# 64-key score blocks, half-height turns and row-wise q and k loads in a fused attention kernel

## The chip, the cores and the metric

The kernel runs on one core of a Trainium2 chip. The time is the device time of one launch in microseconds. The kernel before takes 263.98 us, the median of three runs (263.66 to 265.17).

## The reference

Two attentions in a row, over 8 batches of 576 tokens. The first has 8 heads of 64 and lets a token see only tokens at most 32 away. Its result, 512 wide, is the input of a mixture of four causal attentions ("experts", head width 64) of which each token uses the best two, weighted by a gate.

```python
scores = scale * np.matmul(q, k.transpose(0, 1, 3, 2))
mask = np.abs(pos[:, None] - pos[None, :]) <= window      # window = 32
attn = softmax(np.where(mask, scores, -1e9))
x = (attn @ v)                                            # B, S, 512
logits = x @ w_gate;  topk = best 2 of 4;  w = softmax over the two
for e in range(4):
    q, k, v = x @ wq[e], x @ wk[e], x @ wv[e]
    ye = causal_softmax(scale * q @ k.T) @ v @ wo[e]
    out += (w of e, 0 where e is not chosen) * ye
```

## The kernel before

The program is straight-line code. `ORDER` is a written list of 917 steps; each step has a name, digits for its place in the work (batch first), sometimes a letter after a colon for the engine or the layout, and after an @ the PSUM banks that it uses. A step adds its instructions to the ends of the queues of its engines, so the list is the order on each engine. Semaphores between the engines are put in for the data. A load (`load`, line 184) also waits on its queue until the last TensorE product ahead of it in the list has run, so that a load cannot start earlier than its place.

The steps of the first attention for batch b, head group g (four heads) and half of the queries (288 each):

- `lq`, `lk` load q and k of four heads into a tile of 128 partitions (32 for each head) by 18 tokens by 64. `lv` and `vc` load and copy v.
- `tq`, `tk` (function `turn`, line 288) turn them with VectorE in blocks of 32x32 (line 298), so that the 64 head dimensions lie on partitions as two halves `dh` of 32, for each of four heads: 4 x 32 partitions, tokens along the row. The letters e and f stand for another layout that the list before does not use; t is the layout of the others, issued on ScalarE's queue.
- `sc` (line 323) makes the scores, transposed: keys on partitions, queries along the row, only the blocks that the window touches (`BLK`). Each product has 32 rows of the array (one head, one half `dh`), and the four heads use the four row groups side by side. Two products (`dh` 0 and 1) add up in PSUM. A call has four blocks, one of 128 keys and three of 64, so 32 products. Each fp32 product stands in the trace as two MATMUL records and two LDWEIGHTS records: 64 for each call, in 32 calls. A call uses four of the eight PSUM banks.
- `ex` takes the exponential on ScalarE (line 336, two for each call), `mk` multiplies by the window's mask on VectorE or GpSimd (line 340), `av` multiplies by v, `un` divides by the sums.
- `xt` (line 376) turns the result with TensorE through an identity matrix, in pieces of 128x128, 18 for each batch. `xf` copies it out of PSUM and `xb` casts it to bf16.

The steps of the mixture: `ga`, `gt`, `ge`, `gm`, `gu` are the gate, with small VectorE operations of 20 elements; `pp`/`pe` and `pv`/`ve` the projections and their copies, `ps`/`xe`/`se` scores, exponential and causal mask, `po`/`oe` the product with v, `pt`/`ot` another turn with TensorE (five for each call, the last 64x64), `py`/`ye`/`st` the output product, copy and store.

Lines 179 and 182 are the helpers that issue every product and every TensorE turn, lines 171 and 173 the copies and casts on ScalarE and on VectorE or GpSimd, line 185 every load.

Of the kernel before, what the change touches and what calls it, by code (L numbers as in the profile page):

```python
# [33 lines left out]
    lq200 lk200 xf02:a@0 xb02:v mk1001:g ex1110@4 xt00@6 xf00:a@6 sc110@04 ga0@6 gt0@6 xb00:a ex1101@4 lv10  # L34
    pp001@2 lv12 ex1100@0 mk1100:g lv11 lq210 pp000@0 pe000:v@0 pe001:a@2 pp010@2 pe010:v@2 mk1101:g mk1111:g
    ps003@0 ps000@4 xe003@0 se003 ps002@6 pv00@0 xe000@4 xe002@6 pp011@4 tq200 vc11:g ve00:a@0 pe011:a@4 ps001@6
    xe001@6 tk200 sc200@02 ex2001@2 ps013@4 lv14 xe013@4 mk1110:v lk210 vc10:v lk300 ps010@6 xe010@6 ex2000@0 ge0
    mk2000:g sc201@24 se000 ex2011@4 ex2010@2 se001 ps012@6 tq210 av12@0 mk2011:g un12@0 av10@4 mk2010:g lq300
    pv01@3 xe012@6 ve01:a@3 gm0 lk310 av13@6 av11@0 un10@4 un13@6 un11@0 se012 av14@4 un14@4 tk210 xt11@6 lw3
    xf11:a@6 lv23 xb11:g xt12@0 xf12:v@0 xb12:g xt10@4 lv22 mk2001:g xf10:v@4 xb10:v lv20 ps011@2 xe011@2 sc211@06  # L40
    ex2111@6 ex2110@0 mk2110:v se002 sc210@24 pp110@6 ex2100@2 mk2100:g ex2101@4 lv21 lq310 cw3:g pe110:a@6 gu0
    mk2101:g pp101@2 pe101:a@2 po00@6 pp100@2 tk300 lv24 oe00@6 pp111@4 se011 pt00@6 pe100:v@2 ps102@2 ps103@0
    pe111:a@4 xe102@2 xe103@0 tq300 ga1@7 gt1@7 lq400 ot00:a@6 mk2111:v sc301@24 ex3010@2 ex3011@4 ge1 tk310
    sc300@06 ex3001@6 ps100@2 xe100@2 lk400 tq310 vc21:g se010 av23@4 vc20:g av22@6 un23@4 ex3000@0 pv11@2 un22@6
    ve11:a@2 av20@0 un20@0 av24@7 lk410 un24@7 se013 ps111@4 xe111@4 mk3011:g ps101@2 lv31 xe101@2 av21@0 un21@0
# [12 lines left out]
    xb31:g pp300@4 pt10@0 pp310@6 se211 st02 pt11@1 ot11:a@1 tk600 mk5000:g vc50:g pp301@2 pe301:a@2 xt42@1
    pe310:v@6 pe300:v@4 av42@6 un42@6 av43@2 un43@2 xf42:v@1 st00 ot10:a@0 gm3 py12@0 se203 ye12:a@0 se213
# [28 lines left out]
    ye50:v@0 st50 ps711@6 xe711@6 se711 st51 pv70@2 gu7 pt61@4 ot61:v@4 se703 ve70:a@2 pt60@7 pv71@6 py52@5  # L88
    ye52:a@5 ps710@0 st52 xe710@0 se702 se713 ot60:v@7 py60@2 ye60:a@2 st60 ve71:v@6 po70@6 se710 po71@0 py61@2
    oe70@6 ye61:a@2 pt70@7 st61 py62@6 ye62:a@6 oe71@0 pt71@0 ot71:a@0 ot70:v@7 py70@0 ye70:a@0 py71@6 py72@5 st62  # L90
    ye71:a@6 st70 st71 ye72:v@5 st72
"""


@with_exitstack
def kernel(
# [63 lines left out]
    def two(b0):  # L160
        return PS[:, b0:b0 + 2, :]
# [468 lines left out]
```

## Time and profile before

| | |
|---|---|
| median of three runs | 263.98 us |
| the profiled execution, in all | 264.25 us |
| its span, first to last instruction | 262.5 us |
| TensorE products busy | 228.9 us |
| VectorE busy | 193.2 us |
| ScalarE busy | 147.0 us |
| GpSimd busy | 127.2 us |
| DMA queue of the loads and stores, share of 16 engines | 64.4% |

The profile names the engines PE (TensorE products), PEld (its weight loads), DVE (VectorE), ACT (ScalarE), POOL (GpSimd) and SP (the engine that issues most transfers). A group line gives code line, engine, operation, written and read tiles, shapes, count, then busy time and the mean time of one in ns, then idle time ahead of it and what ended it. For TensorE the shape is rows of the array times columns of the array, then partitions by streamed columns. Busy times of a group count overlapping instructions once, so the mean times count of many products is more than their busy time. A table of stretches gives, for each stretch of the span, its length, the busy time and count of each engine, the granted TensorE clock (1.00 is full), the mean busy share of the DMA engines and GB/s.

### The profile page before, as it was taken

To read this page: it belongs to the slowest core of one execution; us is meant where nothing else is said; L and a number is where in the kernel's file an instruction comes from. 1 tells how busy PE (TensorE), PEld (TensorE's weight loads), DVE (VectorE), ACT (ScalarE), POOL (GpSimd) and SP (SyncE) were. 2 spreads that over 40 slices of the span, in tenths; PEclk is the share of its full clock that TensorE was granted. 3 is DMA by queue.
4 is the path that set the end of the run, shared out by engine and by line. 5 is a ranking of instruction groups with operands and counts; after the bars stand their busy time and mean duration, and the time that the engine had idled before them with its cause. 6 is when DMAs were issued, how large, how long until landed. Compare 5 with 4: busy or idle time off the path is not lost.

```text
span 262.5 us, 11479 instructions
## 1 busy us (share of the span) xinstructions
PE 228.9 (87%) x5013; PEld 183.2 (70%) x5024; DVE 193.2 (74%) x400; ACT 147.0 (56%) x221; POOL 127.2 (48%) x165
## 2 busy tenths in 40 slices
PE   0286999985989999699989999998899989999981
PEld 0165898664768888567878877886688758877650
DVE  2455896759899889998997956986876596667640
ACT  0223416761646557326745677776657657785852
POOL 5019706765686097337967906109734236322400
PEclk9995699999999999999999999999999999999997
DMA  8969989999974598886186798990021520124366
GB/s 166 209 171 180 228 160 211 204 198 226 199 177 138 161 209 176 170 196 162 34 205 201 157 162 159 216 290 15 2 63 42 186 80 2 32 92 157 126 216 208
DMA packets 89362, 40.60 MB, mean 155 GB/s; under 512 B 47072, under 2 KB 84960, under 8 KB 89312
## 3 DMA queue, kind: packets, MB, share of 16 engines
q1 hardware_dynamic: 86752, 38.69, 64.4%
q10 hardware_dynamic: 2560, 1.18, 2.4%
q8 instruction: 39, 0.64, 1.1%
q14 instruction: 11, 0.09, 0.1%
HBM read 30.42 MB, written 9.44 MB: 152 GB/s over the span
## 4 chain that ended last, share of the span: by engine, by line
PE 64%; DVE 16%; DMA 9%; issue 3%; ACT 3%; SPq 2%; POOL 1%; ACTq 0%; DVEq 0%
PE PS L179 57%; PE PS L182 7%; DVE A L340 5%; DMA qn<-in_q_dram 4%; DMA kn<-in_k_dram 4%; SPq L185 2%; ACT A L336 2%; DVE Tkn L298 1%; DVE RG L545 1%; DVE OE L546 1%; DMA out_dram<-Y 1%; DVE XN L368 1%; POOL V L173 1%; DVE Tqn L298 1%; DVE VE L173 1%
## 5 line engine op out<-in xcount | busy, mean ns | idle before, releaser
L179 PE MATMUL PS<-Tqn,Tkn 32*64 32x96 f32 (+5 forms) x2048 | 63.6, 307 | 16.9 <-DVE Tqn L298 11.6
L340 POOL TENSOR_TENSOR A<-A,MASKP 128x576 f32<-128x576 f32 x41 | 59.2, 1458 | 33.1 <-ACT A L336 32.5
L179 PEld LDWEIGHTS PS<-Tqn,Tkn 32*64 32x64 f32 (+1 forms) x2048 | 51.9, 158 | 29.4 <-DVE Tqn L298 12.0
L336 ACT ACTIVATE A<-PS 128x576 f32<-128x576 f32 x64 | 38.9, 650 | 41.0 <-PE PS L179 41.0
L506 ACT ACTIVATE ATE<-PS 128x1024 bf16<-128x1024 f32 x48 | 47.4, 1023 | 8.4 <-PE PS L179 6.8
L511 POOL TENSOR_SCALAR_AFFINE_SELECT ATE<-ATE 128x256 bf16<-128x256 bf16 (+1 forms) x80 | 31.4, 413 | 39.6 <-ACT ATE L506 24.2
L179 PE MATMUL PS<-V,A 128*64 128x65 f32 (+1 forms) x1280 | 39.6, 222 | 3.8 <-DVE XN L368 2.4
L179 PEld LDWEIGHTS PS<-V,A 128*64 128x64 f32 (+1 forms) x1280 | 36.1, 132 | 7.5 <-DVE XN L368 2.9
L173 POOL COPY V<-V 64x2048 f32<-64x2048 f32 (+1 forms) x12 | 21.8, 1820 | 27.3 <-DMA V<-in_v_dram 21.9
L298 DVE STREAM_TRANSPOSE Tkn<-kn 128x576 f32<-128x576 f32 (+2 forms) x36 | 23.2, 686 | 8.4 <-DMA kn<-in_k_dram 7.3
L298 DVE STREAM_TRANSPOSE Tqn<-qn 128x576 f32<-128x576 f32 (+2 forms) x36 | 23.2, 686 | 7.6 <-DMA qn<-in_q_dram 6.6
L340 DVE TENSOR_TENSOR A<-A,MASKP 128x576 f32<-128x576 f32 x23 | 25.3, 1109 | 3.0 <-ACT A L336 3.0
L368 DVE TENSOR_TENSOR XN<-PS,RC 128x512 f32<-128x512 f32 x32 | 22.1, 691 | 1.1
L179 PE MATMUL PS<-WV,XTB 128*128 128x256 bf16 (+1 forms) x192 | 18.8, 255 | 1.1 <-DVE OTT L173 0.8
L179 PE MATMUL PS<-WO,OTT 128*128 128x512 bf16 (+1 forms) x85 | 18.2, 341 | 1.4 <-ACT OTT L171 0.7
L179 PE MATMUL PS<-XTB,WK 128*128 128x288 bf16 x128 | 18.3, 286 | 1.0 <-DVE QKE L173 1.0
L182 PE MATMUL PS<-ident,XN 128*128 128x128 f32 x144 | 18.1, 275 | 1.1 <-DVE XN L373 0.9
L171 ACT COPY Y<-PS 128x1024 f32<-128x1024 f32 (+1 forms) x17 | 13.7, 826 | 9.3 <-PE PS L179 8.3
L179 PE MATMUL PS<-XTB,WQ 128*128 128x288 bf16 x128 | 18.1, 287 | 0.0
L179 PE MATMUL PS<-QKE 64*128 64x64 bf16 (+4 forms) x192 | 16.8, 277 | 1.4 <-DVE QKE L173 1.2
L182 PEld LDWEIGHTS PS<-ident,XN 128*128 128x128 f32 x144 | 15.8, 141 | 3.1 <-DVE XN L373 1.7
L179 PEld LDWEIGHTS <-ATE 128*128 128x128 bf16 x480 | 16.4, 97 | 2.2 <-POOL ATE L511 0.8
(71 smaller groups left out, 279.8 us busy)
## 6 DMA issues: line engine op xcount, KB each, us to landing
V<-in_v_dram SPq DMA_DIRECT2D x32, 256.0 KB, 4.7
out_dram<-Y SPq DMA_DIRECT2D x16, 512.0 KB, 3.8
qn<-in_q_dram SPq DMA_DIRECT2D x56, 144.0 KB, 4.3
kn<-in_k_dram SPq DMA_DIRECT2D x56, 144.0 KB, 4.3
V<-in_v_dram SPq DMA_DIRECT2D x8, 128.0 KB, 4.2
out_dram<-Y SPq DMA_DIRECT2D x16, 64.0 KB, 2.6
kn<-in_k_dram ACTq DMA_DIRECT2D x8, 80.0 KB, 3.5
qn<-in_q_dram SPq DMA_DIRECT2D x8, 80.0 KB, 2.8
```

What stands on the lines that cost most here:

```text
L171: nc.scalar.copy(o, i)
L173: eng(c).tensor_copy(o, i)
L179: last_pe[0] = nc.tensor.matmul(*a, **kw)
L182: last_pe[0] = nc.tensor.transpose(*a)
L185: r = q_.dma_start(o, i)
L298: nc.vector.transpose(T[:, 64 * m0:64 * m1].rearrange("q (m p o) -> q m o p", p=32, o=2), n_[:, 2 * m0:2 * m1, 32 * dh:32 * dh + 32].rearr ...
L336: nc.scalar.activation(AT[(2 * b + g) % NAT_][half][p], two(b0)[:, :, 0:HS], EXP, scale=scale_att)
L340: eng(c).tensor_tensor(out=ap, in0=ap, in1=MASK[:, None, HS * half:HS * half + HS].to_broadcast([128, 2, HS]), op=MULT)
L368: nc.vector.tensor_tensor(out=XN[T // 2][:, T % 2, :].rearrange("p (g h d) -> p g h d", g=2, h=4), in0=u[:, :, :, 0:64], in1=rc[:, :, :, N ...
L506: nc.scalar.activation(chunk(A, ch), two(b0), EXP, scale=scale_moe)
L511: nc.gpsimd.affine_select(ap, ap, pattern=[[0, n], [1, w]], compare_op=IS_GE, fill=0.0, base=0, channel_multiplier=-1)
L545: nc.vector.tensor_tensor(out=rg, in0=GG[b % 2][:, 2 * j:2 * j + 2, :], in1=rg, op=MULT)
```

## The change

Five things change together.

1. `sc`: all blocks have 64 keys, five for each call and so 40 products (80 MATMUL records). Products for the lower half of the partitions (`par` 0) and for the upper half (`par` 1) alternate in an order written out in `SEQ`. Each half of the array columns streams 288 queries for each `dh`.
2. q is loaded in rows of 16 tokens for each partition, with the last 64 tokens in a second transfer of two tokens each (letter x). Its turn is one VectorE instruction of 1,024 elements for each partition and one of 128. The turned q lies in an order (a, p, c), with token 16p + 2a + c, and `sc` reads its queries through that order (`tokens`): pairs of tokens side by side, the next pair 72 elements on.
3. k is loaded in rows of 18 tokens, one transfer of 4,608 bytes for each partition (letter e, or f on ScalarE's queue for batch 0). Its turn is two instructions of 576 elements that write with a step of 18 elements.
4. `xt` turns pieces of 64 partitions by 128, two for each piece of before, into two PSUM banks; `xf` copies from there. The last turn of `pt` is a full 128x128 one.
5. The list is another order of the same 917 steps, with other banks. Letters move some copies: on VectorE `pe` goes from 14 to 9, `xb` from 7 to 1, `xf` from 12 to 10, `ye` from 7 to 4, `ve` from 5 to 4, `ot` from 8 to 11, `mk` from 23 to 25. On ScalarE `pe` goes from 18 to 23, `ye` from 17 to 20, `xf` from 12 to 14, `ot` from 8 to 5. On GpSimd `xb` goes from 10 to 15 and `mk` from 41 to 39.

```diff
@@ -25,70 +25,71 @@
 ORDER = """
-    s_mask s_pads lq100 lk011:t tk011:t lk001:t tk001:t lq011 lq001 tq011 lq002 lk012:t lk002:t lq012 s_ones
-    sc010@02 lv02 lk100 lv01 lv03 s_warm tq001 sc000@46 ex0101@2 ex0001@6 mk0001:g ex0000@4 lv00 s_ident mk0101:g
-    tk002:t tk012:t tq002 sc001@24 ex0011@4 mk0011:g mk0000:g tq012 sc011@46 ex0111@6 tq100 tk100 mk0111:g lq110
-    ex0100@0 ex0110@4 vc00:v ex0010@2 mk0010:v lk110 sc101@06 mk0110:v ex1011@6 tq110 ex1010@0 mk1010:v lv04 lw1
-    sc100@24 vc01:g av02@0 tk110 lv13 ex1001@4 un02@0 mk0100:g av01@4 un01@4 av00@6 un00@6 lw0 ex1000@2 mk1000:v
-    cw0:g av03@2 av04@0 mk1011:g un04@0 sc111@46 un03@2 ex1111@6 cw1:v xt02@0 lw2 cw2:g xt01@2 xf01:v@2 xb01:v
...
+    s_pads s_ones lq012:x lk011:f tq012:x tk011:f lq011:x tq011:x lk012:f tk012:f lk002:f tk002:f lq001:x s_ident
+    tq001:x lq002:x lk001:f lv01 sc010@02 s_warm ex0101@2 lq100:x sc011@46 tq002:x ex0111@6 s_mask mk0111:g
+    lk100:e tk001:f sc000@26 ex0001@6 mk0001:v mk0101:g lv00 ex0100@0 ex0110@4 mk0110:v ex0000@2 mk0100:g lk110:e
+    mk0000:g sc001@06 tk100:e lv03 ex0010@0 mk0010:g lk200:e lv02 tq100:x sc100@02 ex0011@6 mk0011:g ex1001@2
+    vc00:a tk110:e lv04 lq110:x lw1 vc01:g sc101@46 ex1010@4 mk1001:v ex1000@0 lq200:x tk200:e tq110:x ex1011@6
+    av03@2 un03@2 av00@0 un00@0 av01@6 un01@6 av04@4 un04@4 lw0 cw1:g av02@2 un02@2 sc111@06 xt00@4 ex1110@0
+    tq200:x lw2 mk1011:g ex1111@6 xt02@2 lv11 xf02:a@2 xb02:a xt01@0 xf01:v@0 xb01:g sc110@26 cw0:v xf00:a@4
+    xb00:a lv12 ex1101@6 mk1101:v cw2:g ga0@4 gt0@4 ex1100@2 mk1111:v mk1100:g lv13 ge0 pp000@0 lv14 pp001@2
+    pe000:v@0 lv10 vc11:g sc200@46 ex2000@4 pe001:v@2 pp010@0 pe010:v@0 mk1010:v ps002@4 lq210:x gm0 ex2001@6
+    mk2001:g ps001@2 xe001@2 lk210:e vc10:g pp011@6 pe011:a@6 pv00@0 xe002@4 lv22 sc201@26 ve00:a@0 ex2010@2
...
@@ -125,7 +126,9 @@
     PS = psum.tile([128, 8, 512], F32, name="PS")
     NAT = {nm: many(NNAT, [128, 18, 64], F32, nm) for nm in ("qn", "kn")}
 
-    QKT = {nm: [many(2, [128, S], F32, f"T{nm}{g}") for g in range(2)] for nm in ("qn", "kn")}
+    QKT = {nm: many(2, [128, 2, S], F32, "T" + nm) for nm in ("qn", "kn")}
+
+    LAY = {}
     VSB = many(2, [128, 8, H, 65], F32, "V")
 
     AT = [[many(2, [128, 2, HS], F32, f"A{i}{h}") for h in range(2)] for i in range(NAT_)]
@@ -263,21 +266,23 @@
         copy(c, WO, WST[3].rearrange("p (j x) -> p j x", x=512))
 
 
-    PARTS = [(0, 9), (0, 5), (5, 9)]
 
     def load_qk(nm, src, b, g, part, c):
         t = NAT[nm][(2 * b + g) % NNAT]
-        queue = nc.scalar if c in ("f", "t") else nc.sync
+        queue = nc.scalar if c in ("f", "y") else nc.sync
+        s_ = src[b, 4 * g:4 * g + 4]
         if c in ("e", "f"):
             o0, o1 = ((0, 18), (0, 9), (9, 18))[part]
             load(t[:, o0:o1, :].rearrange("p o d -> p (o d)"),
-                 src[b, 4 * g:4 * g + 4].rearrange("h (p o) d -> (h p) o d", o=18)[:, o0:o1, :].rearrange("p o d -> p (o d)"),
+                 s_.rearrange("h (p o) d -> (h p) o d", o=18)[:, o0:o1, :].rearrange("p o d -> p (o d)"), queue)
+        else:
+            o0, o1 = ((0, 16), (0, 8), (8, 16))[part]
+            load(t[:, o0:o1, :].rearrange("p o d -> p (o d)"),
+                 s_[:, 0:512, :].rearrange("h (p o) d -> h p o d", o=16)[:, :, o0:o1, :].rearrange("h p o d -> h p (o d)"),
                  queue)
-        else:
-            m0, m1 = PARTS[part]
-            for h in range(4):
-                load(t[32 * h:32 * h + 32, 2 * m0:2 * m1, :].rearrange("p (m o) d -> p m (o d)", o=2),
-                     src[b, 4 * g + h].rearrange("(m p o) d -> p m (o d)", p=32, o=2)[:, m0:m1, :], queue)
+            if part != 1:
+                load(t[:, 16:18, :].rearrange("p o d -> p (o d)"),
+                     s_[:, 512:576, :].rearrange("h (p o) d -> h p (o d)", o=2), queue)
 
     def lq(c, b, g, part):
         load_qk("qn", q, b, g, part, c)
@@ -286,23 +291,35 @@
         load_qk("kn", k, b, g, part, c)
 
     def turn(nm, b, g, part, c):
-        n_ = NAT[nm][(2 * b + g) % NNAT]
-        for dh in range(2):
-            T = QKT[nm][g][dh]
-            if c in ("e", "f"):
-                o0, o1 = [(0, 18), (0, 9), (9, 18)][part]
-                nc.vector.transpose(T[:, :].rearrange("q (p o) -> q o p", o=18)[:, o0:o1],
-                                    n_[:, o0:o1, 32 * dh:32 * dh + 32])
-            else:
-                m0, m1 = PARTS[part]
-                nc.vector.transpose(T[:, 64 * m0:64 * m1].rearrange("q (m p o) -> q m o p", p=32, o=2),
-                                    n_[:, 2 * m0:2 * m1, 32 * dh:32 * dh + 32].rearrange("p (m o) d -> p m o d", o=2))
+        n_, T = NAT[nm][(2 * b + g) % NNAT], QKT[nm][g]
+        x = n_[:, :, :].rearrange("p o (h d) -> p h o d", h=2)
+        if c in ("e", "f"):
+            LAY[nm, g] = "s"
+            o0, o1 = [(0, 18), (0, 9), (9, 18)][part]
+            for dh in range(2):
+                nc.vector.transpose(T[:, dh, :].rearrange("q (p o) -> q o p", o=18)[:, o0:o1], x[:, dh, o0:o1, :])
+        else:
+            LAY[nm, g] = "m"
+            t = T[:, :, :].rearrange("q h (a p c) -> q h a c p", a=8, c=2)
+            a0, a1 = [(0, 8), (0, 4), (4, 8)][part]
+            nc.vector.transpose(t[:, :, a0:a1, :, 0:32],
+                                x[:, :, 2 * a0:2 * a1, :].rearrange("p h (a c) d -> p h a c d", c=2))
+            if part != 1:
+                nc.vector.transpose(T[:, :, :].rearrange("q h (a p c) -> q h c p a", a=8, c=2)[:, :, :, 32:36, :],
+                                    x[:, :, 16:18, :].rearrange("p h c (i a) -> p h c i a", a=8))
 
     def tq(c, b, g, part):
         turn("qn", b, g, part, c)
 
     def tk(c, b, g, part):
         turn("kn", b, g, part, c)
+
+    def tokens(nm, g, r, dh, lo, hi):
+        T = QKT[nm][g][r, dh, :]
+        if LAY[nm, g] == "s":
+            return T[:, lo:hi]
+        assert nm == "qn"
+        return T.rearrange("r (a p c) -> r p a c", a=8, c=2)[:, lo // 16:hi // 16, :, :]
 
     def lv(c, b, m):
         t = VSB[b % 2]
@@ -317,20 +334,23 @@
             copy(c, pairs[0:64, 0:3, 1], pairs[0:64, 1:4, 0])
 
 
-    BLK = [[(0, 1, 128, 96, 288), (0, 0, 64, 0, 96), (1, 0, 64, 0, 160), (0, 2, 64, 224, 288)],
-           [(0, 2, 128, 288, 416), (0, 3, 64, 352, 480), (1, 3, 64, 416, 576), (0, 4, 64, 480, 576)]]
+    BLK = [[[(0, 0, 96), (1, 96, 224), (2, 224, 288)], [(0, 0, 160), (1, 160, 288)]],
+           [[(2, 288, 352), (3, 352, 480), (4, 480, 576)], [(2, 288, 416), (3, 416, 576)]]]
+
+    SEQ = [[(0, 2, 0), (0, 2, 1), (1, 1, 0), (0, 0, 0), (1, 1, 1), (0, 0, 1), (1, 0, 0), (0, 1, 0), (1, 0, 1), (0, 1, 1)],
+           [(0, 0, 0), (0, 0, 1), (1, 0, 0), (0, 2, 0), (1, 0, 1), (0, 2, 1), (1, 1, 0), (0, 1, 0), (1, 1, 1), (0, 1, 1)]]
 
     def sc(c, b, g, half, b0, b1):
-        Q, K = QKT["qn"][g], QKT["kn"][g]
         bank = (b0, b0 + 1, b1, b1 + 1)
         c0 = HS * half
-        for par, m, n, lo, hi in BLK[half]:
+        for par, i, dh in SEQ[half]:
+            m, lo, hi = BLK[half][par][i]
             k0 = 128 * m + 64 * par
-            for dh in range(2):
-                for hh in range(4):
-                    r = slice(32 * hh, 32 * hh + 32)
-                    mm(PS[64 * par:64 * par + n, bank[hh], lo - c0:hi - c0], K[dh][r, k0:k0 + n], Q[dh][r, lo:hi],
-                       start=(dh == 0), stop=(dh == 1), skip_group_check=True)
+            for hh in range(4):
+                r = slice(32 * hh, 32 * hh + 32)
+                mm(PS[64 * par:64 * par + 64, bank[hh], lo - c0:hi - c0],
+                   tokens("kn", g, r, dh, k0, k0 + 64), tokens("qn", g, r, dh, lo, hi),
+                   start=(dh == 0), stop=(dh == 1), skip_group_check=True)
 
     def ex(c, b, g, half, p, b0):
         nc.scalar.activation(AT[(2 * b + g) % NAT_][half][p], two(b0)[:, :, 0:HS], EXP, scale=scale_att)
@@ -374,23 +394,27 @@
                                     in0=u[:, :, 0:64], in1=rc[:, 0, :, None].to_broadcast([128, 4, 64]), op=MULT)
 
     def xt(c, b, w, b0):
+
         for i in range(2 if w < 2 else 1):
             for dt in range(NDT if w < 2 else 2):
-                turn_pe(PS[:, b0 + i, 128 * dt:128 * dt + 128],
-                        XN[w][:, i, 128 * dt:128 * dt + 128] if w < 2 else XN2[:, 128 * dt:128 * dt + 128], ident)
+                for s in range(2):
+                    r = slice(64 * s, 64 * s + 64)
+                    at = 256 * i + 64 * dt
+                    turn_pe(PS[:, b0 + s, at:at + 64],
+                            XN[w][r, i, 128 * dt:128 * dt + 128] if w < 2 else XN2[r, 128 * dt:128 * dt + 128], ident[r, r])
 
     ENDS = ((0, 32, 0), (9, 0, 544))
 
     def xf(c, b, w, b0):
         F = XTF[b % len(XTF)]
         if w < 2:
-            copy(c, F[:, 1 + 4 * w:5 + 4 * w, :, :].rearrange("p (i s) t x -> p i t s x", s=2),
-                 two(b0).rearrange("p i (t s x) -> p i t s x", s=2, x=64))
+            copy(c, F[:, 1 + 4 * w:5 + 4 * w, :, :].rearrange("p (i s) t x -> p s i (t x)", s=2),
+                 two(b0).rearrange("p s (i y) -> p s i y", i=2))
         else:
 
             for e, (blk, at, _) in enumerate(ENDS):
                 copy(c, F[:, blk, :, at:at + 32].rearrange("p (g t) x -> p g t x", g=2),
-                     one(b0)[:, 0:256].rearrange("p (t g e x) -> p e g t x", t=2, g=2, x=32)[:, e])
+                     two(b0)[:, :, 0:128].rearrange("p g (t e x) -> p e g t x", t=2, x=32)[:, e])
 
     def xb(c, b, w):
         F, W = XTF[b % len(XTF)], XTB[b % 2]
@@ -548,10 +572,8 @@
 
     def pt(c, b, j, b0):
         o = one(b0).bitcast(BF16)
-        O = OE[(2 * b + j) % NOE]
         for t in range(NQT):
-            w = 128 if t < 4 else 64
-            turn_pe(o[:, 128 * t:128 * t + w], O[0:w, t, :, :].rearrange("p e d -> p (e d)"), ident_bf[0:w, 0:w])
+            turn_pe(o[:, 128 * t:128 * t + 128], OE[(2 * b + j) % NOE][:, t, :, :].rearrange("p e d -> p (e d)"), ident_bf)
 
     def ot(c, b, j, b0):
         copy(c, OTT[b % 2][:, j, 0:S], one(b0).bitcast(BF16)[:, 0:S])
```

More of the change, by code (lines that the diff above doesn't have):

```diff
@@ new lines @@
+    ve20:a@0 pp211@2 pe211:a@2 sc501@46 ex5010@4 sc500@02 ex5011@6 lk510:e ga3@4 ps203@6 ex5001@2 se103 vc41:g
+    ex5000@0 gt3@4 gm3 ps211@2 ps202@0 se110 lv44 xe203@6 lk600:e mk4111:g xb32:g xe202@0 lv53 se100 po10@6
+    xe211@2 oe10@6 xb30:g ge3 xb31:g pp300@4 ps212@0 pe300:a@4 tk510:e ps210@2 mk4100:g xe212@0 av41@6 un41@6
+    mk4010:g av40@4 un40@4 mk4011:g av43@0 un43@0 mk5010:g xe210@2 se210 pv21@2 se113 se201 mk5000:g ve21:a@2
+    se211 se202 lv51 py02@7 ye02:a@7 av44@6 lv54 sc510@24 ex5100@2 mk5100:g ex5101@4 pp311@0 pe311:a@0 lq600:x
@@ L92 @@
+    st52 ye51:a@4 st51 oe61@0 pt61@0 ot61:v@0 pt60@7 ot60:v@7 se713 se700 se701 gu7 po70@2 oe70@2 py60@4 se710
+    se712 po71@6 oe71@6 py62@0 ye60:a@4 st60 py61@1 ye62:a@0 st62 pt70@0 ot70:v@0 pt71@7 ot71:v@7 ye61:a@1 st61
+    py70@0 ye70:a@0 st70 py72@7 ye72:a@7 st72 py71@2 ye71:a@2 st71
 """
```

105 lines of the change are left out of this document (47 added, 58 removed).

## Prediction

> **What bounds the kernel now.** I read the page's first two parts, then a table of stretches cut at list places, then the waits of TensorE.
>
> ```profile
> span 262.5 us, 11479 instructions
> PE 228.9 (87%) x5013; PEld 183.2 (70%) x5024; DVE 193.2 (74%) x400; ACT 147.0 (56%) x221; POOL 127.2 (48%) x165
> PEclk9995699999999999999999999999999999999997
> PE 64%; DVE 16%; DMA 9%; issue 3%; ACT 3%; SPq 2%; POOL 1%; ACTq 0%; DVEq 0%
> ```
>
> ```profile
> core 0: us, PE busy (x) PEld busy (x) DVE busy (x) ACT busy (x) POOL busy (x), PEclk, DMA share, GB/s
> 0.00:11.64 11.64, 0.00 (x0) 0.00 (x0) 4.29 (x23) 0.28 (x1) 3.87 (x12) 1.00 0.94 185
> 11.64:42.24 30.60, 27.41 (x694) 23.24 (x698) 22.51 (x40) 11.56 (x20) 14.79 (x13) 0.83 0.89 187
> 42.24:78.65 36.41, 30.95 (x651) 24.13 (x651) 28.05 (x49) 19.22 (x32) 24.66 (x26) 1.00 1.07 203
> 78.65:125.95 47.30, 44.62 (x1119) 36.61 (x1117) 42.41 (x81) 26.11 (x42) 25.68 (x28) 1.00 0.75 170
> 125.95:174.92 48.97, 48.03 (x1071) 39.47 (x1069) 39.66 (x82) 33.13 (x51) 25.55 (x32) 1.00 0.79 175
> 174.92:218.80 43.88, 40.82 (x890) 31.94 (x891) 32.85 (x64) 27.62 (x43) 22.22 (x31) 1.00 0.25 74
> 218.80:257.00 38.20, 37.09 (x603) 27.82 (x606) 23.03 (x62) 28.24 (x39) 10.44 (x27) 1.00 0.33 112
> 257.00:262.50 5.50, 0.00 (x0) 0.00 (x0) 0.42 (x1) 0.82 (x1) 0.00 (x0) 0.76 0.60 215
> ```
>
> ```profile
> PE PS L179 <- DVE Tqn L298: 11.6, 1, 11.6
> PE PS L179 <- ACT A L336: 3.5, 4, 1.3
> ```
>
> From 78.65 us on TensorE is the bound: 92.65 us busy of 96.27 up to 174.92. But VectorE has 82.07 us of work there, and in the stretch from 78.65 to 125.95 it is at 0.90. Whatever is taken from TensorE alone stops paying after some 10%. Ahead of 78.65 the transfers are the second bound: their share is 0.94, 0.89 and 1.07, TensorE waits 11.6 us for its first turned q, and between 42.24 and 78.65 it stands for 5.46 us. The clock row is low in its fourth and fifth slice, 20 to 33 us; I count calls there at the full-clock price, so the gain there is rather more. The reader is to see three regimes: transfers, then two engines close together, then (from 218.80) TensorE alone.
>
> **The change, part by part.**
>
> *Score calls.*
>
> ```profile
> 78.66 3.46 PE L179 MATMUL PS<-Tqn,Tkn 32*128 32x128 f32 x128
> 80.32:81.18 0.86, 0.86 (x19) 1.00 0.61 171
> 81.18:82.04 0.86, 0.86 (x52) 1.00 0.28 73
> 84.52 1.83 PE L179 MATMUL PS<-V,A 128*64 128x65 f32 x64
> ```
>
> Two calls take 3.46 us, so 1.73 each. The second one splits in two: 0.86 us for the 128-key block (16 records), 0.86 us for the three 64-key blocks (48 records and the seams). The third row gives the streaming price: two `av` calls, 64 records on two column halves, 32 in sequence of 65 columns, 1.83/2080 = 0.88 ns for a column. The 128-key block streams 4 x 192 columns, 0.68 us by that price, so 0.18 us goes to the start; the 64-key blocks stream 4 x 160 in each half, 0.56, so 0.30 goes to the change of shape and the drain. After: one shape, 4 x 288 columns in each half, 1.01 us, and one seam of 0.18 to 0.30, none between two calls in a row. I take 1.25 us: -0.48 for each of 32 calls, -15.4 us. The ends: 1.05 us (no seam), and 1.43 if the records and not the columns set the pace, since the 48 records of 64 keys needed 0.86 us, 18 ns each, and there will be 80. If the two halves don't run side by side it is 2.27. They do in the row: two halves of 0.56 in turn don't fit in 0.86.
>
> The Trainium skill, page "TensorE: Matmul & The Clock Gate", section "Wait — 56ns, not 53.3ns?", says that matmuls do not start closer than about 25 ns however small they are. By that rule 80 records take 2.0 us, slower than now. The 18 ns of the row above speaks against it for products on different parts of the array.
>
> *Turns of x.*
>
> ```profile
> 226.54 2.13 PE L182 MATMUL PS<-ident,XN 128*128 128x128 f32 x18
> 226.32 2.10 PEld L182 LDWEIGHTS PS<-ident,XN 128*128 128x128 f32 x18
> L182 PE MATMUL PS<-ident_bf,OE 128*128 128x128 bf16 x64 | 6.2, 220 | 0.7 <-DVE OE L546 0.6
> L182 PE MATMUL PS<-ident_bf,OE 64*128 64x64 bf16 x16 | 3.2, 200 | 0.0
> L179 PE MATMUL PS<-Tqn,Tkn 32*128 32x192 f32 x16 | 0.9, 347 | 0.0
> ```
>
> A batch's 18 turns take 2.13 us. After there are 36 with half the columns, on two row groups. Side by side they take half and a start, 1.18: -0.95 for each batch, -7.6 us. If the weight loads, as long as the products (2.10), went one after the other, 36 would take 4.2: +2.1 for each batch. I take side by side, by the last row: 16 records of 347 ns on four row groups fit in 0.9 us. The last `pt` turn goes from 3.2/16 = 0.20 to 6.2/64 = 0.10: -1.6 us. TensorE: 228.9 - 24.6 = 204.3 us.
>
> *Turns of q and k, and moved copies.*
>
> ```profile
> L298 DVE STREAM_TRANSPOSE Tkn<-kn 128x576 f32<-128x576 f32 x28 | 20.0, 754 | 3.8 <-DMA kn<-in_k_dram 2.7 <-PE PS L179 1.1
> L298 DVE STREAM_TRANSPOSE Tqn<-qn 128x320 f32<-128x320 f32 x4 | 1.8, 492 | 3.5 <-DMA qn<-in_q_dram 3.5
> 240.30 0.18 DVE L440 TENSOR_TENSOR NU<-EX,PK 128x20 f32<-128x20 f32 x1
> 240.95 0.20 DVE L443 TENSOR_TENSOR G<-NU,su 128x20 f32<-128x20 f32 x1
> L173 DVE CAST QKE<-PS 128x576 bf16<-128x576 f32 x14 | 10.4, 749 | 3.8 <-PE PS L179 3.0 <-ACT VE L171 0.7
> L173 DVE CAST XTB<-XTF 128x1024 bf16<-128x1024 f32 x3 | 3.8, 1265 | 1.6 <-ACT XTF L171 1.5
> L340 DVE TENSOR_TENSOR A<-A,MASKP 128x576 f32<-128x576 f32 x23 | 25.3, 1109 | 3.0 <-ACT A L336 3.0
> ```
>
> 754 against 492 ns for 256 elements more gives 1.02 ns an element and 0.17 us fixed. q: 1,024 and 128 elements, 1.21 + 0.30, against 2 x 0.75 now: nothing, +1 us in all for the small one's wide steps. k keeps 2 x 576 elements but writes with a step of 18 elements (72 bytes) where it now writes with 2. No such turn is in the trace. One end is 754 again. The other comes from the gate's small operations: `G`, which writes with a step of 5 elements, takes 0.20 us where `NU`, which writes in a row, takes 0.18, both of 20 elements: +1 ns an element, 1.33 us for a turn. I take the dear end, because `G` is the only row whose writes skip: +1.16 for each of 14 full turns and +2.4 on the four half ones, +18.6 us.
>
> The Trainium skill, page "SBUF — State Buffer", section "Specifications (TRN2)", says that the memory works in lines of 16 bytes and needs two hits on a line for full rate. By it the k turns are the dear ones, the sum below; by the 754 ns row alone it is the cheap case further down.
>
> The copies that move take from VectorE 5 x 0.749 + 3 x 1.265, and two masks bring 2 x 1.109: -5.3 us. The other letters (ends of batches, `xf`, `ye`, `ot`) I put at -4 together. VectorE: 193.2 + 18.6 + 1 - 9 = 203.8 us. ScalarE takes the five `pe` casts, some 4 us at VectorE's price, and GpSimd four full `xb` casts for two masks less: both are under 0.75 busy in every stretch of the table.
>
> *Loads.*
>
> ```profile
> q1 hardware_dynamic: 86752, 38.69, 64.4%
> qn<-in_q_dram SPq DMA_DIRECT2D x56, 144.0 KB, 4.3
> GB/s 0 0 0 0 0 0 147 212 311 319 275 203 171 186 246 243 214 210 205 254 224 232 220 198 196 196 253 237 202 191 200 215 236 203 181 212 193 229 196 173
> ```
>
> The GB/s row cuts the first 12 us in 40: nothing moves before 1.8 us, then some 215. Four transfers of 512-byte rows become one or two with rows of 4 KB, and SP issues 48 instead of 128 for q and k. In the stretches a full share carries 185/0.94 = 197 GB/s at the start and 215/0.60 = 358 in the tail, where only the stores' 2 KB rows move. The first call now needs both parts of q and of k of one group, 1.18 MB, because a row of 18 tokens crosses all key blocks: by 358 GB/s landed at 5.2 us, with the loads of the other group between, 6. The turns (0.99 + 1.5 + 0.69 + 1.5 us, from 3.5) end at about 8.3. First product at 8.3 instead of 11.64: -3.3. Loads are also moved in the list, and those queued behind a late one on SP wait with it; with 80 issues less on that queue I put this at nothing; if SP falls behind, the 5.46 us of standing between 42 and 79 come back.
>
> **The sum**, for each stage the later of TensorE and VectorE, VectorE filled to 0.94, which is what TensorE reaches where it is the bound:
>
> - To 78.65: TensorE -3.3 (start) - 5.8 (12 calls) - 1.9 (two batches of turns) - 2.7 (half of the 5.46) leaves 65.0. VectorE has 4.29 + 22.51 + 28.05 + 8.2 (k) + 0.5 - 3 = 60.6, of it 2.5 before the turns begin at 3.5: 3.5 + 58.1/0.94 = 65.3. Gain 13.3.
> - 78.65 to 174.92 (14 calls, four batches, 8 k turns): TensorE 92.65 - 11.1 = 81.6, at 0.96 filled 85. VectorE 82.07 + 9.3 + 0.4 - 4.5 = 87.3, /0.94 = 92.9. Gain 3.4: here the cover is gone, and VectorE is late next.
> - 174.92 to 218.80 (6 calls): TensorE 40.82 - 4.0 = 36.8, /0.94 = 39.1. Gain 4.8.
> - 218.80 to the end: 1.2.
>
> 264.25 us (the profiled execution, span 262.5 and 1.75 around it) - 22.7 = 241.5; the median of the runs is 0.27 below it: 241.
>
> **The rivals.**
>
> *Cheap k turns.* They cost 754 ns as now; then TensorE bounds the middle: 11 us gained there instead of 3.4, in all -31: 233. For it: all turns of the trace have one price for an element. Against it: the `G` row.
>
> *A price on TensorE is not reached.* Half turns in sequence (+24 us of TensorE against the sum): gains 7.6, -1.4, 1.5, -1.9 by the same stages: 258. Or the floor for each record, 2.0 us a call: 4.7 + 0.4 + 0 + 1.2: 258. At 18 ns a record (1.43) VectorE hides most: 243.
>
> *Slower: the query stream.* `sc` now reads its queries in pairs, each 72 elements from the last. No product of the trace streams so; the shortest runs are 32 elements, in the gate. If pairs stream at half rate, a call takes 2.02 + 0.25 = 2.27 us, +1.02 against the sum: to 78.65 the gain shrinks to 1.4, the middle takes 95.9/0.96 = 99.9 (+3.6), the next 42.9/0.94 = 45.7 (+1.8), the end -1.2: +2.8, 267. It decides from 2.19 us a call. For it speaks that VectorE's skipping `G` is dearer; against it only that the products' price of 0.88 ns for an element leaves a reader time. By the Trainium skill's rule on lines of 16 bytes (the page and section named above) a pair is two hits on a line and streams at full rate; no run here shows it.
>
> *No gain.* The new list may bring its own waits, as ScalarE's 3.5 us above, that eat what TensorE saves; the two engines at 204 us each must fit in one span. With a filling of 0.84 instead of 0.94 the stages become 72.7, 103.9, 43.8 and -1.2: with the tail 263 us of span, 264.
>
> **How the numbers follow.** Dear k turns 0.42 (235 to 249), cheap ones 0.25 (229 to 237), a TensorE price missed 0.18 (about 258), query stream 0.10, no gain 0.05. The likeliest gives 241. The range 230 to 262 leaves out the query stream and the best of the cheap cases, under 2 in 10. A change of 0.5% is about what measuring this kernel can tell from none: faster 0.85, same 0.04, slower 0.11.
>
> **What would show it.** Two score calls in a row at 2.1 to 2.6 us, not 3.46; a batch's x turns at 1.2; `Tkn` turns at 1.3 us; first product near 8 us; VectorE ahead of TensorE from 79 to 175. Score calls at 2 us or more, or a first product after 12, would make it wrong.

## The result and the profile after

The changed kernel takes 307.1 us, the median of four runs (305.8 to 309.4), against 264.5 us for four runs of the kernel before (263.7 to 265.2). The ratio is 1.162, interval 1.154 to 1.170: slower, where I forecast 241 us and a range of 230 to 262. Here and below, runs that took over 1.5% longer than the fastest run of their kernel are left out of the ratios.

From the page of the kernel after: the span, the engines, and the queue of the loads and stores.

```profile
span 307.7 us, 12651 instructions
PE 226.9 (74%) x5671; PEld 179.1 (58%) x5680; DVE 193.7 (63%) x381; ACT 151.3 (49%) x234; POOL 128.8 (42%) x169
q1 hardware_dynamic: 56648, 38.68, 48.6%
```

TensorE is busy for 2.0 us less than before (228.9) and idle for 80.8 us of the span where it was idle for 33.6. So the whole loss, 45.2 us of span, is idle time. VectorE has no more work than before (193.7 against 193.2). The transfers move the same 38.7 MB and their share fell from 64.4% to 48.6%: no engine is full and the transfers look idle.

VectorE's wait for q in the kernel before (total, times, longest, in us):

```profile
DVE Tqn L298 <- DMA qn<-in_q_dram: 6.6, 4, 2.0
```

The waits of VectorE and of TensorE in the kernel after:

```profile
DVE Tqn L305 <- DMA qn<-in_q_dram: 43.8, 14, 6.9
PE PS L182 <- DVE Tkn L300: 22.1, 6, 14.4
PE PS L182 <- DVE Tqn L305: 8.3, 1, 8.3
```

The first row is the answer's outline: VectorE, about to turn q, stands for 43.8 us for q's transfer, nearly as much as the kernel lost, where it was 6.6 us before. TensorE then waits for the turns, 14.4 us for the first. The stretches of the kernel after, the columns as in the table of before:

```profile
0.00:14.43 14.43, 0.00 (x1) 0.00 (x1) 5.70 (x26) 1.49 (x2) 4.53 (x15) 1.00 0.54 149
14.43:60.00 45.57, 25.38 (x836) 21.80 (x836) 23.21 (x34) 13.57 (x23) 13.31 (x10) 0.70 0.58 134
100.00:150.00 50.00, 37.84 (x1050) 31.72 (x1055) 33.43 (x56) 21.16 (x32) 27.30 (x27) 0.83 0.52 121
```

Where the kernel before had a DMA share of 0.89 to 1.07 in its first 79 us, the share is now between 0.5 and 0.6 in the stretches shown, while the engines wait for those transfers. A queue that is needed and yet half empty is the sign to look for here: it suggests that each transfer is slow by itself. The idle TensorE also got a lower clock, 0.70 in the second row, so its work got longer too.

The groups and two stretches of the timeline (start and length in us) that price the parts of the change:

```profile
L300 DVE STREAM_TRANSPOSE Tkn<-kn 128x576 f32<-128x576 f32 x28 | 32.6, 1242 | 6.7 <-DMA kn<-in_k_dram 6.7
L305 DVE STREAM_TRANSPOSE Tqn<-qn 128x1024 f32<-128x1024 f32 x14 | 17.4, 1242 | 35.3 <-DMA qn<-in_q_dram 35.3
L185 PE MATMUL PS<-ident,XN 64*128 64x64 f32 x288 | 12.5, 238 | 0.0
L185 PE MATMUL PS<-ident_bf,OE 128*128 128x128 bf16 x80 | 6.6, 220 | 0.5 <-DVE OE L570 0.5
L308 DVE STREAM_TRANSPOSE Tqn<-qn 128x128 f32<-128x128 f32 x16 | 6.0, 374 | 1.1 <-DMA qn<-in_q_dram 1.0
```

```profile
14.43 4.93 PE L182 MATMUL PS<-Tqn,Tkn 32*64 32x64 f32 x160 [14.43 <-DVE Tkn L300]
213.22 2.67 PE L182 MATMUL PS<-Tqn,Tkn 32*64 32x64 f32 x160
```

Two score calls in a row take 2.67 us, 1.34 each, where two took 3.46. The k turns take 1,242 ns where they took 754.

### The profile page after: what moved, and what is told of

The parts are those of the page before. It is cut to its first block, busy times and chain, and to the rows that moved or that the text cites. A ratio compares the mean times of both kernels' runs of the same rounds, so it can differ in the third digit from the quotient of the medians.

```text
span 307.7 us, 12651 instructions
## 1 busy us (share of the span) xinstructions
PE 226.9 (74%) x5671; PEld 179.1 (58%) x5680; DVE 193.7 (63%) x381; ACT 151.3 (49%) x234; POOL 128.8 (42%) x169
## 3 DMA queue, kind: packets, MB, share of 16 engines
q1 hardware_dynamic: 56648, 38.68, 48.6%
## 4 chain that ended last, share of the span: by engine, by line
DMA 45%; PE 33%; DVE 12%; issue 3%; POOL 2%; ACT 2%; SPq 2%; DVEq 0%; ACTq 0%; POOLq 0%
PE PS L182 31%; DMA qn<-in_q_dram 21%; DMA out_dram<-Y 8%; DMA V<-in_v_dram 8%; DMA kn<-in_k_dram 8%; DVE Tkn L300 3%; DVE Tqn L305 2%; PE PS L185 2%; ACT Y L174 1%; POOL V L176 1%; DVE RG L569 1%; DVE OE L570 1%; POOL A L360 1%; SPq L608 1%; SPq L188 1%
## 5 line engine op out<-in xcount | busy, mean ns | idle before, releaser
L182 PE MATMUL PS<-Tqn,Tkn 32*64 32x128 f32 (+3 forms) x2560 | 56.3, 313 | 34.6 <-DVE Tkn L300 22.1
L182 PEld LDWEIGHTS PS<-Tqn,Tkn 32*64 32x64 f32 x2560 | 46.0, 157 | 42.1 <-DVE Tkn L300 19.8
L360 POOL TENSOR_TENSOR A<-A,MASKP 128x576 f32<-128x576 f32 x39 | 57.6, 1489 | 23.5 <-ACT A L356 23.1
L182 PE MATMUL PS<-V,A 128*64 128x65 f32 (+1 forms) x1280 | 46.6, 241 | 18.7 <-DMA V<-in_v_dram 6.9
L182 PEld LDWEIGHTS PS<-V,A 128*64 128x64 f32 (+1 forms) x1280 | 42.1, 148 | 24.3 <-issue 13.8
L305 DVE STREAM_TRANSPOSE Tqn<-qn 128x1024 f32<-128x1024 f32 (+1 forms) x18 | 20.2, 1124 | 43.8 <-DMA qn<-in_q_dram 43.8
L300 DVE STREAM_TRANSPOSE Tkn<-kn 128x576 f32<-128x576 f32 (+1 forms) x36 | 37.4, 1120 | 6.7 <-DMA kn<-in_k_dram 6.7
L182 PE MATMUL PS<-VE,ATE 128*128 128x65 bf16 x480 | 17.9, 195 | 9.6 <-POOL ATE L535 9.6
L182 PE MATMUL PS<-QKE 64*128 64x64 bf16 (+4 forms) x192 | 18.3, 285 | 4.3 <-DVE XN L388 4.2
L176 POOL CAST XTB<-XTF 128x1024 bf16<-128x1024 f32 (+1 forms) x19 | 13.8, 750 | 17.2 <-DVE XTF L176 11.4
```

The source lines that it names most:

```text
L176: eng(c).tensor_copy(o, i)
L182: last_pe[0] = nc.tensor.matmul(*a, **kw)
L300: nc.vector.transpose(T[:, dh, :].rearrange("q (p o) -> q o p", o=18)[:, o0:o1], x[:, dh, o0:o1, :])
L305: nc.vector.transpose(t[:, :, a0:a1, :, 0:32], x[:, :, 2 * a0:2 * a1, :].rearrange("p h (a c) d -> p h a c d", c=2))
L360: eng(c).tensor_tensor(out=ap, in0=ap, in1=MASK[:, None, HS * half:HS * half + HS].to_broadcast([128, 2, HS]), op=MULT)
```

## Experiments

The suspects for the slow transfers were three. A: q's transfer works with few DMA engines. Its source is four heads of 32 rows of 4 KB each; the first 512 of 576 tokens of a head don't join on to the next head, so the outermost dimension of the source is 4, while k's, whole heads, is one dimension of 128 rows. In the packets of the trace, a q transfer of the kernel after is 128 packets of 4,096 bytes that take 6.1 to 9.5 us. In the mean of a transfer 3.0 to 3.9 of them are under way at a time; of k's 4,608-byte packets it is 3.5 to 12. B: long rows are slow as such. C: the places of the loads in the list, or SP's queue, are late.

The Trainium skill, page "DMA: Bandwidth & Descriptors", section "Why a DMA increments its semaphore by 16 and not by 1", says that a transfer uses the largest number of engines up to 16 that divides the slowest dimension of both its sides; by that rule q gets 4. The packets of the trace agree with it.

*q by head.* Four transfers of 32 rows, the same rows, turns, products and list:

```diff
-            load(t[:, o0:o1, :].rearrange("p o d -> p (o d)"),
-                 s_[:, 0:512, :].rearrange("h (p o) d -> h p o d", o=16)[:, :, o0:o1, :].rearrange("h p o d -> h p (o d)"),
-                 queue)
+            for h in range(4):
+                load(t[32 * h:32 * h + 32, o0:o1, :].rearrange("p o d -> p (o d)"),
+                     s_[h, 0:512, :].rearrange("(p o) d -> p o d", o=16)[:, o0:o1, :].rearrange("p o d -> p (o d)"),
+                     queue)
```

> The changed kernel with one edit: the 16-token rows of q are loaded as four transfers of 32 partitions (one for each head) in place of one of 128 partitions whose source begins with a dimension of 4 heads. Same rows of 4 KB, same places in the list, three more issues on SP for each load. Theory A (a transfer whose source begins with 4 uses 4 of the 16 DMA engines; in the changed kernel 128 packets of 159 to 290 ns take 6 to 9.5 us, 3.0 to 3.9 at a time): a q load takes 1.5 to 3 us, VectorE's wait for q falls from 43.8 us to under 8, the time to 240 to 258. Theory B (long rows as such are slow, or hold up what is behind them): no change, 300 to 312. Theory C (the new list places the loads too late, or SP falls behind): no gain or slower by the added issues, 303 to 315.

Measured: 261.0 us (259.1 to 264.2), 0.983 of the kernel before, interval 0.974 to 0.991. One edit of one transfer takes 46 us away, and the kernel is then 0.9 to 2.6% faster than the one before. Its page:

```profile
PE 215.3 (83%) x5671; PEld 170.1 (66%) x5680; DVE 198.5 (77%) x381; ACT 151.5 (58%) x234; POOL 129.8 (50%) x169
q1 hardware_dynamic: 57728, 38.69, 54.7%
```

Its waits:

```profile
DVE Tqn L306 <- DMA qn<-in_q_dram: 9.5, 6, 4.6
PE PS L182 <- DVE Tkn L301: 12.2, 1, 12.2
PE PS L182 <- issue: 5.9, 6, 1.9
```

The wait for q falls from 43.8 to 9.5 us. Theory A had expected somewhat more, 240 to 258 us and a wait under 8. TensorE is busy for 11.6 us less with the same products: its mean granted clock is 0.952 where it was 0.886. The start is not won back: the first product comes at 12.2 us. SP now issues 18 transfers of q ahead of its first load of v, which takes it 11.9 us; whether that holds up the start was not tested.

*q by two heads.* The dose the other way: two transfers of two heads, so that the outermost dimension is 2. Rows and bytes are the same, and there are fewer issues than by head.

```diff
-            for h in range(4):
-                load(t[32 * h:32 * h + 32, ...
+            for h in (0, 2):
+                load(t[32 * h:32 * h + 64, ...
```

> The changed kernel with the 16-token rows of q as two transfers of two heads each, so that each source begins with 2. Theory A: only two engines carry all q rows, 16 loads of 512 KB at about 24 GB/s for each engine are 173 us on those two beside their share of the rest: one look at 350 to 430 us, packets of q 2 at a time. Theory B: as the changed kernel, 300 to 312. Theory C: one issue more for each load, 303 to 312.

Measured, one run: 383.2 us. The queue on its page, and VectorE's wait for q:

```profile
q1 hardware_dynamic: 56648, 38.68, 36.3%
```

```profile
DVE Tqn L306 <- DMA qn<-in_q_dram: 101.4, 15, 10.6
```

With an outermost dimension of 32, 4 and 2 the kernel takes 261, 307 and 383 us, and VectorE waits 9.5, 43.8 and 101.4 us. Neither rows nor list differ, so B and C fall as the cause. (C would make the variant by head, with the most issues, the slowest.) The packets go with the time: of q's, some 1.7 to 2.0 are under way at a time with two heads, and 3.7 to 12.3 by head, where a transfer of 32 rows takes 0.5 to 2.3 us.

The traces also let the engines be counted. Each of the four k transfers on ScalarE's queue leaves 16 packets of 4 bytes beside its data. On SP's queue there are 1,608 such packets in the kernel after, 1,608 with two heads and 2,688 by head. That is what 4, 2 and 16 for each q transfer give: 18 x 4 and 36 x 2 are both 72, and 72 x 16 is 1,080 more.

*The 64-token tail by head too.* This transfer also starts with 4 heads; eight transfers for a load instead of five.

> As q_by_head, and the last 64 tokens of q too as one transfer for each head, so eight transfers for each q load. Theory A: the small transfer (64 KB on 4 engines) is worth little, within 3 us of q_by_head, and the four more issues on SP (about 0.45 us each) may take that back: 240 to 260. Theories B and C: as the changed kernel or slower, 303 to 320.

Measured: 268.2 us (266.3 to 271.3), ratio 1.013, interval 1.008 to 1.017. That is outside what theory A expected, 240 to 260. The 64 KB tail was not what was late, and with three more issues on SP's queue for each load the kernel takes 7 us more than the variant above.

*q in rows of 18 tokens, as k.* Letter e for x in the list: one transfer of 128 rows, two turns with wide steps, queries read in a row.

> The changed kernel with q loaded and turned like k: one transfer with rows of 18 tokens, whose heads and rows merge into one dimension of 128, two turns of 576 elements with a write step of 18, and score products that read their queries in a row and not in pairs. Theory A: q loads take 2 to 4 us, VectorE's wait for q falls under 10 us, VectorE gets 16 x 0.9 us more work: 245 to 265. Theory B: rows are even longer (4.6 KB), no gain: 300 to 315. Theory C: one issue less for each load, but the same places: 295 to 310. Rival on the query stream: if pairs cost the products time, a warm score call is shorter here than the 1.34 us of the changed kernel; if pairs are free, 1.30 to 1.36.

Measured: 262.2 us (257.1 to 266.8), the two shortest runs 257.1 and 259.3. The profiled run is the shortest, with a span of 255.4 and a mean granted clock of 0.991; the clocks of the others are 0.940 to 0.963. Its page, two waits of TensorE, and a lone call in its timeline:

```profile
PE 212.5 (83%) x5671; PEld 167.5 (66%) x5680; DVE 205.6 (81%) x383; ACT 151.3 (59%) x234; POOL 130.5 (51%) x169
```

```profile
PE PS L182 <- DVE Tkn L300: 9.2, 1, 9.2
PE PS L182 <- issue: 8.9, 11, 2.4
```

```profile
41.01 1.36 PE L182 MATMUL PS<-Tqn,Tkn 32*64 32x64 f32 x80
```

A lone call in the timeline of the kernel after:

```profile
56.78 1.41 PE L182 MATMUL PS<-Tqn,Tkn 32*64 32x64 f32 x80
```

Reading the queries in pairs costs 0.05 us a call. The first product comes at 9.2 us: with 128 rows outermost and one issue for each load the start is near what I forecast.

So the loss is explained. But 261 is not 241, and the second question is where the rest of the gain went.

*TensorE's edits alone, on the kernel before.* The old list, loads and turns of q and k, with only the 64-key blocks (`BLK`, `SEQ` and the loops of `sc` as in the change), only the half-height x turns of the full pieces, or both.

> The kernel before with nothing changed but the score products: 64-key blocks in the new order, 80 records a call; its loads, turns of q and k, x turns and list stay. Theory E (TensorE's saved time comes back where TensorE is the bound): a call 1.73 -> about 1.3 us, 32 calls, 13.8 us less on TensorE (page: 215), and by my stages 9 to 13 us of it in the time: 251 to 255. Theory F (list, banks and transfers were laid out for the old durations, and the next wait takes the gain): TensorE's busy time falls all the same, but the time stays at 260 to 265, with the difference standing in new waits of TensorE for ScalarE's copies, VectorE's turns or transfers.

> The kernel before with only the x turns changed, and only the 16 full ones of each batch: 32 turns of 64 partitions by 128 into two banks, and the copy that reads them. Theory E: 2.13 -> about 1.3 us a batch, 8 batches, 6.5 us less on TensorE (page: 222), 3 to 6 us of it in the time: 258 to 261. Theory F: 263 to 265. If half turns ran one after the other: 4 us a batch and 275 to 280.

> Both TensorE edits together on the kernel before: no new load, no new turn of q or k, no new list. This is the part of the change that I priced as a gain, without the part priced as a loss. Theory E: TensorE's busy time 229 -> about 208, time 243 to 252, which beats both kernels and the two variants with good q loads (261, 262), so that the rest of the missing gain lies in the dear turns, the loads and the list. Theory F: 257 to 264, so that the 20 us taken from TensorE cannot come back whole without a list of their own.

Measured: 267.5, 265.0 and 267.0 us; the ratios are 1.013 (1.006 to 1.020), 1.006 (1.002 to 1.010) and 1.013 (1.007 to 1.019). Cheaper products bring the old kernel nothing; by the intervals they cost it 0 to 2%. With the 64-key blocks the time lies above what either theory expected. TensorE's wait without a releaser in the kernel before, and the page and the same wait with the 64-key blocks:

```profile
PE PS L179 <- issue: 0.2, 1, 0.2
```

```profile
PE 220.7 (83%) x5525; PEld 177.5 (67%) x5536; DVE 190.6 (71%) x400; ACT 146.9 (55%) x221; POOL 127.1 (48%) x165
```

```profile
PE PS L179 <- issue: 9.7, 11, 2.0
```

TensorE is busy for 8.2 us less and idle for 12.5 us more of the span (46.1 against 33.6). Of that, 9.5 us are waits with no releaser in the trace ("issue"). These pauses have a pattern. Those at 82.65, 89.98 and 101.98 us come after 3,501, 4,011 and 4,523 TensorE records: 510 and 512 apart. Each ends 1.45 to 1.50 us after a 16,384-byte packet of the instruction queue has landed. Theory G: they are waits for code. A packet holds 256 of TensorE's instructions (the kernel before has 39 of them for 10,037 records), and in none of these traces do two packets start less than 3.2 us apart (the closest are 3.26). An old call is 128 instructions (64 MATMUL and 64 LDWEIGHTS records) in 1.73 us; a new one is 160 in 1.34, which needs 256 in 2.1 us.

*Each score call three times in a row*, in the kernel before and in the one with the 64-key blocks, with the same loop around both:

```diff
+        for rep in range(3):
```

> The kernel before with every score call issued three times in a row (the same result three times): 64 calls more, 64 records (128 instructions) each. Theory G (the pauses of TensorE behind no release are waits for its next block of code: a block holds 256 of its instructions, and the blocks of the traces come at least 3.4 us apart): 128 instructions take at least 1.7 us, which a call takes anyway. Theory E (a call costs its busy time): 64 x 1.73 = 111 us. Both: about 375 us, or 10 to 20 less where the added calls fill idle time.

> The kernel before with the 64-key score blocks, and every score call three times in a row: 64 calls more, 80 records (160 instructions) each. Theory E: 64 x 1.3 = 83 us on the 267 us of one call each, at most 350, some 25 us less than the same with the old blocks. Theory G: three calls are 480 instructions, nearly two blocks of code, and take about 2.1 us each however fast the products are: 64 x 2.1 = 137 us, about 390 to 405, slower than the same with the old blocks though each call alone is faster; TensorE's waits without a releaser grow from 9.7 us to 40 or more, in pauses that end some 1.4 us after a 16 KB instruction packet.

Measured: 368.5 us with the old blocks and 405.1 with the new (two runs each, 368.2 to 368.7 and 405.0 to 405.3; ratios to the kernel before 1.389, interval 1.378 to 1.400, and 1.527, interval 1.515 to 1.539). Calls that are cheaper one by one are 36.7 us dearer in a row. Page row, wait and timeline of the old blocks, three times:

```profile
PE 338.6 (92%) x9120; PEld 273.6 (75%) x9120; DVE 189.9 (52%) x400; ACT 147.2 (40%) x221; POOL 124.5 (34%) x165
```

```profile
PE PS L179 <- issue: 2.8, 6, 0.7
```

```profile
189.58 10.25 PE L179 MATMUL PS<-Tqn,Tkn 32*128 32x192 f32 x384
```

And of the new blocks, three times:

```profile
PE 311.4 (77%) x10656; PEld 260.2 (65%) x10656; DVE 186.6 (46%) x400; ACT 147.2 (36%) x221; POOL 124.9 (31%) x165
```

```profile
PE PS L179 <- issue: 67.5, 48, 2.6
```

```profile
196.77 1.25 PE L179 MATMUL PS<-Tqn,Tkn 32*64 32x128 f32 x66
199.90 2.33 PE L179 MATMUL PS<-Tqn,Tkn 32*64 32x128 f32 x128 [1.88 <-issue]
203.63 2.26 PE L179 MATMUL PS<-Tqn,Tkn 32*64 32x160 f32 x128 [1.40 <-issue]
207.36 0.98 PE L179 MATMUL PS<-Tqn,Tkn 32*64 32x128 f32 x46 [1.47 <-issue]
```

128 products with their weight loads, 256 instructions, then a pause; again and again. (The first line is cut by the edge of the view's window.) From 199.90 to 207.36 two blocks take 7.46 us, 3.73 each, of which 2.3 is work. The packets of the trace for these pauses:

| pause, us | records before it | 16 KB packet landed |
|---|---|---|
| 198.02 to 199.90 | 11,176 | 198.39 |
| 202.23 to 203.63 | 11,432 | 202.36 |
| 205.89 to 207.36 | 11,688 | 206.12 |

Theory G holds: the busy time fell by 27 us and the waits for code rose by 65. The old calls run 768 instructions in 10.25 us without a pause, 3.42 us for 256, about as fast as packets come. Whether their pace is set by the code or only happens to equal it, these runs don't tell.

The Trainium skill, page "Runtime: NRT & Kernel Launch", section "Instruction fetch mechanics", says that code is refilled in blocks of 16 KiB, 256 instructions, and that crossing into the next is mostly hidden. The size agrees with the trace. That it is hidden does not, where TensorE runs many short products in a row: 67.5 us in 48 pauses.

*The old blocks in the new list*: the variant with rows of 18, with `BLK` and the loops of `sc` of the kernel before.

> The variant with q in rows of 18 tokens, with the old score blocks (one of 128 keys and three of 64) in place of the new ones: what the score blocks alone are worth in the new list, once loads are good. By my prediction's price, 32 calls x 0.43 us = 14 us, of which the stages let 8 to 14 through: 270 to 276, TensorE busy about 226. Theory G: the new blocks win 14 us of busy time and lose 6 to 9 us of it to code: 265 to 269, and TensorE's waits without a releaser fall from 8.9 us to under 2.

Measured: 263.6 us (261.8 to 265.9), 0.988 of the kernel before, interval 0.980 to 0.996; with the new blocks it was 262.2. Its page, and TensorE's waits without a releaser:

```profile
PE 226.6 (86%) x5168; PEld 178.5 (68%) x5168; DVE 209.4 (80%) x383; ACT 151.6 (58%) x234; POOL 130.5 (50%) x169
```

```profile
PE PS L182 <- issue: 1.4, 3, 0.6
```

The new blocks take 14.1 us from TensorE's busy time, close to the 14 expected, and add 7.5 us of waits for code. (The two profiled runs differ in their granted clock, 0.991 and 0.953, so some of the 14.1 may be clock.) In the time 1.4 us are left by the medians of all runs, and some 4.5 by the shorter ones (257.1 and 259.3 against 261.8 to 264.6). So 10 to 13 us didn't come through, and code stands for 7.5 of them; the rest of the list's slack was not followed further.

*Cheap k turns*, in the variant by head: k's turns write in a row, so that the keys of a call stand in another order. The result is another; the work is the same in all else.

```diff
-                nc.vector.transpose(T[:, dh, :].rearrange("q (p o) -> q o p", o=18)[:, o0:o1], x[:, dh, o0:o1, :])
+                nc.vector.transpose(T[:, dh, :].rearrange("q (o p) -> q o p", p=32)[:, o0:o1], x[:, dh, o0:o1, :])
```

> The variant with four transfers for q, with k's turns writing their tokens in a row instead of 18 elements apart, so that the keys of a call stand in another order (the result is not the reference's; the work is the same in all else). It prices the dear turns alone. The turns: 1242 -> about 754 ns, 28 + 8 of them, 16 us less on VectorE (page: 198.5 -> 182). By my prediction's stages (cheap instead of dear: 241 -> 233) 8 us less: 253. If VectorE's wide-step turns lie beside other work in the list as it is, 258 to 261.

Measured: 258.2 us (256.8 to 260.0), ratio 0.974, interval 0.967 to 0.980. Its page, and the group of k's turns:

```profile
PE 215.5 (83%) x5680; PEld 170.4 (66%) x5680; DVE 185.4 (72%) x381; ACT 151.2 (59%) x234; POOL 130.3 (50%) x169
```

```profile
L301 DVE STREAM_TRANSPOSE Tkn<-kn 128x576 f32<-128x576 f32 x28 | 20.1, 752 | 4.3 <-DMA kn<-in_k_dram 3.8 <-PE PS L182 0.5
```

The same turn takes 752 ns when it writes in a row and 1,242 when it writes 72 bytes apart. 13 us less on VectorE are worth 2.8 us of time, with intervals that overlap: VectorE was mostly not what TensorE waited for.

## Why the prediction was wrong

**Loads: the step that failed.** I put q and k "landed at 5.2 us, with the loads of the other group between, 6" by 358 GB/s, a rate that I had taken from the stores at the end, the first product at 8.3 us, and the loads behind it "at nothing". q's transfers have an outermost dimension of 4, carry 512 KB in 6.1 to 9.5 us, at 55 to 86 GB/s, and the first product came at 14.43. Not the start alone is lost: VectorE stands for 43.8 us for q loads, the last time at 188 us. The step counted bytes, rows and issues, and not the shape of the transfer; and it took longer rows and fewer issues for a gain. No rival had it: the slower one was the query stream. With the one edit the time is 261, at the upper edge of the range, but the first product at 12.2; with 128 rows outermost and one issue it comes at 9.2, near the 8.3.

**The sum: what is taken from TensorE comes back in the time.** This failed too, by the 20 us between 241 and 261: with the loads mended the kernel is near the "no gain" rival (264), to which I gave 0.05. I saw only VectorE and the transfers as the next limit ("stops paying after some 10%"). Code was a third limit: most of the 5.9 to 8.9 us of waits without a releaser in the variants with good loads. What holds the rest stays open. TensorE's busy time, forecast at 204.3 us, is 215.3 by head and 212.5 with rows of 18; four of the eight calls of the first 45 us, which I priced at full clock and expected to gain more, still take 2.4 us each by head. And the old list takes nothing from a cheaper TensorE (1.013). That VectorE "is late next" in the middle stretch was wrong in the size: I took 8 us between dear and cheap turns, and 2.8 were measured. VectorE's work, forecast at 203.8 us, is 198.5 by head.

**Score calls: right.** Predicted 1.73 to 1.25 us, measured 1.34 to 1.41 where queries are read in pairs and 1.29 to 1.36 where they are read in a row. At 1.34 the 32 calls save 12.5 us, where the sum took 15.4. Records go at 2.67/160 = 16.7 ns. The floor of 25 ns that the Trainium skill, page "TensorE: Matmul & The Clock Gate", section "Wait — 56ns, not 53.3ns?", states does not hold here for products on different parts of the array. The rival of a slow query stream fell: 0.05 us a call. But the cheaper call brought the waits for code, which no row of before could show, since it had 0.2 us of them.

**Turns of x: right side, too large.** The half pieces are busy for 12.5 us, 11.9 in the variant with rows of 18, where the full ones were for 18.1: -5.6 to -6.2 against the -7.6 of the sum. They do run side by side. `pt`: 80 x 220 ns, 6.6 us busy where it was 9.4: -2.8 against -1.6.

**Turns of q and k: right side, right size.** Dear k turns, 1.33 predicted, 1.24 measured; q's 1.21 + 0.30 predicted, 1.24 + 0.37 measured. That the k price came out so near is partly luck, since it rested on 0.02 us between two small operations. The trace agrees in both places with the Trainium skill's rule on lines of 16 bytes (page and section named in the prediction): wide-step writes are slow, pairs stream at almost full rate.

## What to carry to other kernels

Before you price a transfer by bytes, look at the outermost dimension of both its sides: a slice that no longer joins heads or batches into 128 rows can leave a handful of DMA engines (four here), and its sign in the profile is a DMA share that falls while engines wait for loads. Count instructions as well as nanoseconds on TensorE: here a run of short products that needs 256 instructions in less than some 3.4 us waits for its code. And test a cheaper part in the list that it will run in, since a list laid out around old durations may give nothing back.

## What was not expected of the hardware

- The same 512 KB of q cost the kernel 261, 307 or 383 us with an outermost dimension of 32, 4 or 2.
- TensorE's code comes in packets of 16 KB, in these traces at least 3.26 us apart, and a pause at a block's border ends some 1.1 to 1.6 us after its packet has landed.
- The mean granted clock fell where TensorE waited more: 0.952 by head, 0.886 in the kernel after, 0.816 with two heads. Between the first two lie 11.6 us of busy time for the same products. No run varied the waiting alone.
- The kernel with three more issues for each q load on SP's queue (the 64-token tail by head) took 7 us more.
